# One remainder unit of 256 columns at the end, in place of two of 128, in a pooled attention with a multiplicative FFN

## The chip, the cores and the metric

The kernel runs on one core of a Trainium2 chip. The core has a matrix engine (TensorE, PE in the profile), a vector engine (VectorE, DVE), a scalar engine for activations (ScalarE, ACT), a general-purpose engine (GpSimd, POOL) and SyncE (SP), which here only issues transfers. Each runs its own instructions in order and waits for the others by semaphores. PE writes to PSUM, eight banks of 2 KB in each of 128 partitions; the other engines read the results from there.

The metric is the device time of one execution in microseconds, lower being better, as the median of several runs.

## The reference

Queries are averaged in neighbouring pairs, so that 1152 become 576. Attention follows, for 8 batches of 8 heads with 64 elements a head. Its output, 8 x 576 = 4608 tokens of 512 elements, goes through an FFN that multiplies two projections:

```
q_pool = q.reshape(B, H, S // 2, 2, D).mean(axis=3)
scores = matmul(q_pool, k.T) / sqrt(D)        # 576 x 1152 for each batch and head
attn   = softmax(scores)
x      = matmul(attn, v)                       # heads joined: (4608, 512)
a, b   = x @ w1, x @ w2                        # (4608, 1024)
out    = ((a * b) @ w3) @ w_out                # (4608, 512)
```

Inputs and output are float32; the kernel computes in float16 with float32 sums.

## The kernel before

**Attention.** Two heads of a batch form a pair P, 32 pairs in all, four to a batch. The scores of all pairs are one long sequence of columns, cut into 324 chunks of 512 columns. `scores(c)` (L294) computes a chunk on PE for both heads, one on each half of PE's rows, into a PSUM tile `psc`. `expo(c)` (L300) takes the exponential on ACT and writes it to the ring `er`. For a pair, `attend(P, u)` (L312) is called twice, once for each head, and multiplies the exponentials with the values. 576 is 4 x 128 + 64: the last 64 tokens of a batch, its remainder, are done for both heads in the call with u = 0 (L321). `normalize` divides and writes the tokens as `xn` (DVE), and SP's transposing DMAs bring them to `xT`, a batch's 512 main tokens. The remainders go through `rems` to `xR[:, head pair, batch // 2, head, 64]`, the even batches on partitions 0 to 63 and the odd ones on 64 to 127.

**FFN.** w3 and w_out are multiplied together once, early (T16, L477), so that the FFN is a gate and a row product. A `unit` is the FFN of a set of tokens. Its gates work on row tiles: h = 0 and h = 1 use the two 64-row halves of PE at once, each on other tokens. For each of 8 column tiles ft and each h, a gate is 16 matmuls of n columns (L514), 8 with w1 and 8 with w2, into one PSUM tile `pg`. Then one half is copied to `asb` (L497 on DVE, or L494 on ACT at the end) and DVE multiplies both into `gT[h]` (L506). The rows follow (L535): for each block of 128 tokens 16 matmuls of 512 columns, 8 on row tile 0 and then 8 on row tile 1, into `pp`, which is scaled into `osb` (L528, or L524 on ACT at the end) and stored by SP (L600). For a unit marked `final` the row blocks are kept back in the list `last` and run after everything else, with all 128 rows of PE at once; the very last block is cut into two halves (`last_rows`, L608).

**Units.** Every batch has a unit with n = 256, its main tokens. Remainders are grouped: with batch 3 comes a unit with n = 128 for the remainders of batches 0 to 3, and with batch 7 one for batches 4 to 7, which is `final`. `add_batch` puts the gates of the two units into one order, four of the main unit first and then mixed.

**Order of the work.** The program text is laid out by a planner in the kernel's own Python, with a model clock for each row tile, costs for each kind of instruction and due times. Chunks of scores come when their due time (the modelled end of the exponential two chunks ahead) is reached. Before that, `step(h)` fills the time with work of the queues `prep[h]` and `ffn[h]`. The FFN of a batch enters its queues once the attention of that batch has been issued, and its gates may start only when the model clock has passed `ready`, 6.5 us after the last u = 0 normalization (8.0 for the first two batches; L334). Row tile 0 may run ahead of row tile 1 by LEAD = 2.6 us of FFN work. The row products hand a PSUM tile from one row tile to the other through a tiny DVE copy (L434). After the last scores and attention blocks, `tail` is set: two more PSUM banks are used and ACT takes over copies. PE executes all of it in this fixed order.

The transfers are in three queues: loads of q, k, v and weights on POOL's, transposes and most stores on SP's, and two of the last stores on ACT's. Besides these, each engine's instructions are fetched by DMA (q8 and q14 in the profile).

Of the kernel before, what the change touches and what calls it, by code (L numbers as in the profile page):

```python
# [8 lines left out]
FP16 = mybir.dt.float16  # L9
# [14 lines left out]
def kernel(  # L24
# [17 lines left out]
    NF = dff // 128  # L42
# [9 lines left out]
    ffp = ctx.enter_context(tc.tile_pool(name="ffp", bufs=2))  # L52
# [4 lines left out]
    xR = const.tile([128, H // 2, 4, 2, 64], FP16)  # L57
# [26 lines left out]
    def vector(n, at):  # L84

        nonlocal vec
        vec = max(vec, at + T_SEM) + 0.16 + n / 960
        return vec
# [7 lines left out]
    def take():  # L96
        return spare.pop(0)[1]
# [311 lines left out]
    w3T = {}  # L409
# [31 lines left out]
    def add(queue, block, cost, ready, emit):  # L441


        for h in block.tiles:
            for n in range(block.n_products):
                queue[h].append((block, n, cost, ready(n) if callable(ready) else ready, emit))
# [34 lines left out]
    def unit(n, x, places, ready, final=False):  # L481

        gT = {}
        gdone = [[[1e9] for _ in range(NF)] for _ in range(2)]
        pairs = places[0][2][0][0] == places[0][2][1][0]

        def gate(ft, h):
            def mul(t, at):  # L490
                asb = ffp.tile([128, 256], FP32, tag="asb", bufs=3, name="asb")
                b, a = t[:, n:2 * n], asb[:, 0:n]
                if tail:
                    nc.scalar.copy(out=a, in_=t[:, 0:n])  # L494
                    at += 0.4
                else:
                    nc.vector.tensor_copy(out=a, in_=t[:, 0:n])  # L497
                    vector(n, at)
                if h not in gT:
                    gT[h] = ffp.tile([128, NF, n], FP16, tag="g" if n == 256 else "w3T",  # L500
                                     bufs=4, name="gT")
                g = gT[h][:, ft, 0:n]
                if pairs:
                    g = g.rearrange("f (i p c) -> f i c p", p=64, c=2)
                    b, a = (y.rearrange("f (i c p) -> f i c p", c=2, p=64) for y in (b, a))
                nc.vector.tensor_mul(out=g, in0=b, in1=a)  # L506
                done = vector(n, at)
                gdone[h][ft][0] = done + T_SEM
                return done
            fs = slice(ft * 128, ft * 128 + 128)  # L510

            def emit(t, s, i, start, stop):
                w, m = divmod(i, H)
                nc.tensor.matmul(t[:, n * w:n * w + n], (w1sb, w2sb)[w][s, (m + h) % 2, m // 2, fs],  # L514
                                 x(s, m),
                                 start=start, stop=stop, skip_group_check=True)
            add(ffn, Block("pg", 2 * H, (h,), mul), 0.0025 + n / 2400,
                [ready, copied[2 * ft // NF]], emit)

        def rows(h, o, places):  # L520
            def store(t, at):
                osb = ffp.tile([128, dm], FP32, tag="osb", bufs=3, name="osb")
                if tail:
                    nc.scalar.activation(out=osb, in_=t, func=AF.Copy, bias=0.0,  # L524
                                         scale=1.0 / (SCL * SCL))
                    done = at + T_SEM + 0.65
                else:
                    nc.vector.tensor_scalar_mul(out=osb, in0=t, scalar1=1.0 / (SCL * SCL))  # L528
                    done = vector(512, at)
                store_rows(osb, places)  # L530
                return done
            cs = slice(o, o + 128)

            def emit(t, s, i, start, stop):
                nc.tensor.matmul(t, gT[h][s, i, cs], T16[s, i, :], start=start, stop=stop,  # L535
                                 skip_group_check=True)
            if final:
                last.append((emit, store, places, lambda i: gT[h][:, i, cs]))
            else:
                add(ffn, Block("pp", NF, (0, 1), store), 0.216,  # L540
                    lambda i: [gdone[h][i]], emit)

        yield gate
        for h, o, to in places:
            rows(h, o, to)

    def add_batch(b, ready):

        k, o, end = (b // 2) % 2, 256 * (b % 2), b == B - 1
        units = [unit(256, lambda s, m: xT[s, m, k, o:o + 256],  # L550
                      [(h, 128 * i, [(b, 4 * i + 2 * h), (b, 4 * i + 2 * h + 1)])
                       for h in range(2) for i in range(2)], ready)]
        if b % 4 == 3:
            units.append(unit(
                128, lambda s, m: xR[s, m // 2, b // 2 - 1:b // 2 + 1, m % 2],
                [(h, 0, [(b - 3 + h, 8), (b - 1 + h, 8)]) for h in range(2)], ready, final=end))
        gates = [next(u) for u in units]
        for h in range(2):
            order = [(ft, gates[0]) for ft in range(NF)]
            for ft in range(NF if len(gates) > 1 else 0):  # L560
                order.insert(4 + 3 * ft // 2, (ft, gates[1]))
            for ft, gate in order:
                gate(ft, h)
        for u in units:
            next(u, None)
# [32 lines left out]
    def store_rows(osb, places):  # L598
        for r, rows in rows_out(places, slice(0, dm)):
            nc.sync.dma_start(out=rows, in_=osb[r])  # L600
# [76 lines left out]
    while c < NCHUNK or bursts or ffn[0] or ffn[1]:  # L677
        h = 0 if clock[0] <= clock[1] else 1
# [7 lines left out]
        if c >= NCHUNK or due(c) > clock[h]:  # L686
            fresh = False
            if c >= NCHUNK and not tail and not bursts:
                tail = True
                spare += [(max(clock), 4), (max(clock), 5)]  # L690
            keep = 1 if prep[0] or prep[1] or bursts and c > bursts[0][0] - 1 else 0
            if not step(h):
                if swap_due():
                    clock[:] = [max(clock) + 0.1] * 2
                    swap_halves()
                    clock[:] = [clock[0] + 0.1] * 2
                else:
                    clock[h] += 0.02
            while ended and not early and not prep[0] and not prep[1]:
                b, ready = ended.pop(0)  # L700
                add_batch(b, ready)
            continue
# [9 lines left out]
        if jobs:  # L712
            n, job = jobs.pop(0)
# [6 lines left out]
        while events and at >= events[0][0]:  # L720
            _, n, act = events.pop(0)
# [14 lines left out]
    for emit, store, _, _ in last[:-1]:  # L736
        n = take()
# [35 lines left out]
```

## Time and profile before

| | before |
|---|---|
| median of 3 runs | 421.24 us (420.91 to 422.11) |
| span of the profiled execution, first to last instruction | 423.3 us |
| PE busy with matmuls | 403.7 us, 7666 matmuls |
| ACT busy | 331.1 us, 308.8 of it with 324 exponentials |
| DVE busy | 218.9 us |
| narrow gates (xR, 128 columns) | 512 matmuls, first at 219.3, last at 406.9 us |
| last attention block on PE ends | 372.8 us |

The profile gives the profiled execution's own time only as its span; it is 2.1 us above the median of the runs, and none of those is named as the one that was profiled. A matmul's duration in the profile (216 ns with 128 columns, 269 with 256) includes its way through the array, and consecutive ones overlap; the pace is read from the starts. "Issue" ahead of an instruction means that the engine stood still though no semaphore that the profile shows was pending.

### The profile page before, as it was taken

The numbers are of one execution on the slowest core, as the hardware profiler recorded it, in microseconds if no ns is written. First come the engines' busy times: TensorE is split into PE (matmuls) and PEld (weight loads), VectorE is DVE, ScalarE is ACT, GpSimd is POOL, SyncE is SP. The second block draws the span as 40 slices with busy tenths as digits, with TensorE's granted clock in tenths as the row PEclk, the third lists the DMA queues.
The fourth block names the chain that finished last, engine by engine and source line by source line (L and its number), as shares of the span: only waits on it lengthen the run. The fifth ranks groups of instructions, "written<-read, shape, count | busy, mean of one in ns | idle before, by whom it ended". The sixth has DMA issues, their size and how long they took to land.

```text
span 423.3 us, 17431 instructions
## 1 busy us (share of the span) xinstructions
PE 403.7 (95%) x7666; PEld 318.0 (75%) x7666; DVE 218.9 (52%) x596; ACT 331.1 (78%) x382; POOL 191.2 (45%) x209
## 2 busy tenths in 40 slices
PE   3799999998999999999999899999999999999996
PEld 1366665777768887888788786788878887888993
DVE  2266656875435653565365663356446644542540
ACT  3968888887788888888888788889888888834432
POOL 8233345860566576555655556665569300000000
PEclk9999999999899999999999999999999999999999
DMA  8999999999699999999999999999996215102004
GB/s 120 206 207 202 186 205 204 189 161 121 110 154 206 152 141 153 196 144 121 192 170 132 139 134 132 190 185 150 137 170 141 42 35 133 43 19 101 4 11 141
DMA packets 94219, 59.02 MB, mean 139 GB/s; under 512 B 64832, under 2 KB 84544, under 8 KB 94144
## 3 DMA queue, kind: packets, MB, share of 16 engines
q0 software_dynamic: 26528, 33.56, 50.7%
q1 hardware_dynamic: 67456, 24.22, 35.1%
q8 instruction: 60, 0.98, 1.0%
q10 hardware_dynamic: 160, 0.13, 0.1%
q14 instruction: 15, 0.12, 0.1%
HBM read 67.11 MB, written 9.44 MB: 181 GB/s over the span
## 4 chain that ended last, share of the span: by engine, by line
PE 93%; ACT 3%; issue 2%; DMA 1%; DVE 0%; POOL 0%; DVEq 0%; ACTq 0%; POOLq 0%
PE pg L514 30%; PE psc L294 19%; PE po L312 18%; PE pp L535 15%; PE pT L477 4%; PE po L321 3%; ACT er L300 3%; PE t L262 1%; PE sw L391 1%; DMA kst<-in_k_dram 1%; PE w3t L465 0%; PE pp L608 0%; PE tb L195 0%; POOL qst L108 0%; ACT kc L207 0%
## 5 line engine op out<-in xcount | busy, mean ns | idle before, releaser
L300 ACT ACTIVATE er<-psc 128x1024 f16<-128x1024 f32 x324 | 308.8, 1030 | 52.0 <-PE psc L294 48.7
L294 PE MATMUL psc<-qT,kT 64*128 64x384 f16 (+7 forms) x1152 | 132.3, 291 | 4.6 <-ACT er L300 3.8
L514 PE MATMUL pg<-xT,w2sb 64*128 64x256 f16 x1024 | 131.3, 270 | 0.0
L514 PE MATMUL pg<-xT,w1sb 64*128 64x256 f16 x1024 | 130.7, 271 | 0.1
L514 PEld LDWEIGHTS <-w1sb 64*128 64x128 f16 x1280 | 97.9, 94 | 10.9 <-issue 2.7
L514 PEld LDWEIGHTS <-w2sb 64*128 64x128 f16 x1280 | 96.7, 94 | 6.2 <-issue 0.4
L535 PE MATMUL pp<-T,gT 64*128 64x512 f16 (+1 forms) x552 | 94.4, 376 | 0.0
L312 PEld LDWEIGHTS <-er 128*128 128x128 f16 x2304 | 74.5, 98 | 17.6 <-issue 15.0
L294 PEld LDWEIGHTS <-kT 64*128 64x128 f16 x1152 | 60.6, 95 | 32.5 <-issue 16.8
L312 PE MATMUL po<-vt,er 128*128 128x65 f16 x2304 | 82.4, 194 | 2.0 <-issue 1.8
L506 DVE TENSOR_TENSOR gT<-pg,asb 128x256 f16<-128x256 f32 (+1 forms) x160 | 66.3, 417 | 20.8 <-ACT asb L494 16.3
L497 DVE COPY asb<-pg 128x256 f32<-128x256 f32 (+1 forms) x119 | 48.0, 404 | 32.1 <-PE pg L514 30.5
L340 DVE RECIPROCAL rz<-po 128x4 f32<-128x4 f32 x64 | 12.1, 189 | 89.7 <-PE po L312 46.0
L143 POOL TENSOR_TENSOR qp<-qst 64x1152 f16<-64x1152 f16 x23 | 54.5, 2370 | 1.0
L535 PEld LDWEIGHTS <-gT 64*128 64x128 f16 (+1 forms) x552 | 41.3, 94 | 13.8 <-issue 0.4
L168 POOL COPY seen<-kT 1x1 f16<-1x1 f16 x19 | 3.4, 180 | 88.0 <-DMA kT<-kc 88.0
L152 POOL COPY vt<-vst 128x1152 f16<-128x1152 f16 x28 | 32.1, 1150 | 4.6 <-issue 3.9
L123 POOL DMA_DIRECT2D vst<-in_v_dram x32 | 23.3, 729 | 17.2 <-DMA kst<-in_k_dram 7.4
L116 POOL DMA_DIRECT2D kst<-in_k_dram x33 | 24.0, 729 | 11.7 <-issue 3.0
L343 DVE TENSOR_TENSOR xn<-po,rz 128x256 f16<-128x256 f32 x64 | 27.2, 424 | 2.2
L494 ACT COPY asb<-pg 128x256 f32<-128x256 f32 (+1 forms) x41 | 12.8, 332 | 19.4 <-PE pg L514 18.9
L161 POOL COPY kc<-kst 128x1152 f16<-128x1152 f16 x23 | 26.9, 1169 | 0.0
(62 smaller groups left out, 256.2 us busy)
## 6 DMA issues: line engine op xcount, KB each, us to landing
qst<-in_q_dram POOLq DMA_DIRECT2D x32, 288.0 KB, 6.0
vst<-in_v_dram POOLq DMA_DIRECT2D x32, 288.0 KB, 8.2
kst<-in_k_dram POOLq DMA_DIRECT2D x31, 288.0 KB, 5.4
out_dram<-osb SPq DMA_DIRECT2D x32, 256.0 KB, 3.2
w3h<-in_moe_w_dram POOLq DMA_DIRECT2D x4, 512.0 KB, 15.6
wosb<-in_moe_w_out_dram POOLq DMA_DIRECT2D x1, 1024.0 KB, 13.8
xT<-xn SPq DMA_TRANSPOSE x64, 5.8
w1sb<-in_moe_w_dram POOLq DMA_DIRECT2D x2, 512.0 KB, 15.9
```

The costliest lines, as they stand in the source:

```text
L116: nc.gpsimd.dma_start(out=kst[P][:, :, js[0]:js[1], :], in_=k[b, h0:h0 + 2].rearrange("u (p j) d -> p u j d", j=NJ)[:, :, js[0]:js[1], :])
L143: (eng or nc.vector).tensor_tensor(out=qps[pp][r].rearrange("p c u d -> p u c d"), in0=src[:, :, :, 0, :], in1=src[:, :, :, 1, :], op=ALU.add)
L152: (eng or nc.vector).tensor_copy(out=vts[P % 4][:, :, :, 0:D], in_=vst.pop(P))
L161: nc.gpsimd.tensor_copy(out=kc.rearrange("p j u d -> p u j d"), in_=kst.pop(P))
L294: nc.tensor.matmul(t[:, u, o:o + ln], kT[P][s, j, :], qv[s, f0:f0 + ln], start=True, stop=True)
L300: nc.scalar.activation(out=er[:, :, r:r + CH], in_=psc.pop(c), func=AF.Exp, bias=0.0, scale=SCALE)
L312: nc.tensor.matmul(po[:, VW * i:VW * i + D + 1], er[:, u, r:r + 128], vts[P % 4][:, u, j, 0:D + 1], start=(j == 0 and i == 0), stop=(j == ...
L343: nc.vector.tensor_tensor(out=xn, in0=acc[:, 0:4, 0:D], in1=rz[:, 0:4].to_broadcast([128, 4, D]), op=ALU.mult)
L497: nc.vector.tensor_copy(out=a, in_=t[:, 0:n])
L506: nc.vector.tensor_mul(out=g, in0=b, in1=a)
L514: nc.tensor.matmul(t[:, n * w:n * w + n], (w1sb, w2sb)[w][s, (m + h) % 2, m // 2, fs], x(s, m), start=start, stop=stop, skip_group_check=True)
L535: nc.tensor.matmul(t, gT[h][s, i, cs], T16[s, i, :], start=start, stop=stop, skip_group_check=True)
```

## The change

The unit of remainders that came with batch 3 is dropped. With batch 7 comes one unit for the remainders of all eight batches, with n = 256. On row tile h its columns are the remainders of batches h, 2 + h, 4 + h and 6 + h. It is marked `final`, so that all its four row blocks are in the list `last`, where there were two. The number of columns, multiplications and output rows is the same. Its `gT` takes buffers of the tag "g", where the narrow units took those of "w3T".

```diff
                 if h not in gT:
-                    gT[h] = ffp.tile([128, NF, n], FP16, tag="g" if n == 256 else "w3T",
-                                     bufs=4, name="gT")
+                    gT[h] = ffp.tile([128, NF, n], FP16, tag="g", bufs=4, name="gT")
...
-        if b % 4 == 3:
+        if end:
             units.append(unit(
-                128, lambda s, m: xR[s, m // 2, b // 2 - 1:b // 2 + 1, m % 2],
-                [(h, 0, [(b - 3 + h, 8), (b - 1 + h, 8)]) for h in range(2)], ready, final=end))
+                256, lambda s, m: xR[s, m // 2, :, m % 2],
+                [(h, 128 * i, [(4 * i + h, 8), (4 * i + 2 + h, 8)])
+                 for h in range(2) for i in range(2)], ready, final=True))
```

## The prediction

> **What bounds the kernel now.** I read the page first: its busy row and its slices say that TensorE (PE) has hardly an idle slice, while the exponentials on ScalarE (ACT) take 78%.
>
> ```profile
> span 423.3 us, 17431 instructions
> PE 403.7 (95%) x7666; PEld 318.0 (75%) x7666; DVE 218.9 (52%) x596; ACT 331.1 (78%) x382; POOL 191.2 (45%) x209
> PE   3799999998999999999999899999999999999996
> q8 instruction: 60, 0.98, 1.0%
> ...
> L514 PEld LDWEIGHTS <-w1sb 64*128 64x128 f16 x1280 | 97.9, 94 | 10.9 <-issue 2.7
> ```
>
> So the question is what PE does when. The chain in order of time shows the end. The last attention block ends at 372.8; all that follows is FFN back to back: the rest of batch 6, then the gates of batch 7 mixed with those of the second remainder unit (387.78 to 406.4 and a little beyond), then output rows.
>
> ```profile
> 371.00 1.39 PE po L312 x40
> 372.80 5.57 PE pg L514 x100
> 380.77 4.61 PE pp L535 x42
> 387.78 18.65 PE pg L514 x382
> 408.79 8.85 PE pp L535 x61
> 417.64 1.76 PE pp L608 x16
> ```
>
> Third, PE's timeline around the first remainder unit (batches 0 to 3, in the FFN of batch 3), with the first gate of batches 4, 6 and 7 on row tile 0.
>
> ```profile
> 226.43 0.22 PE L514 MATMUL pg<-xR,w2sb 64*128 64x128 f16 x1
> 226.44 0.22 PE L514 MATMUL pg<-xR,w1sb 64*128 64x128 f16 x1
> 226.49 0.22 PE L514 MATMUL pg<-xR,w2sb 64*128 64x128 f16 x1
> 226.50 0.22 PE L514 MATMUL pg<-xR,w1sb 64*128 64x128 f16 x1
> ...
> 230.27 0.23 PE L514 MATMUL pg<-xR,w1sb 64*128 64x128 f16 x1 [0.68 <-issue]
> ...
> 242.09 0.23 PE L514 MATMUL pg<-xR,w1sb 64*128 64x128 f16 x1 [1.45 <-issue]
> ...
> 271.16 0.27 PE L514 MATMUL pg<-xT,w1sb 64*128 64x256 f16 x1
> ...
> 352.56 0.27 PE L514 MATMUL pg<-xT,w1sb 64*128 64x256 f16 x1
> ...
> 385.11 0.38 PE L514 MATMUL pg<-xT,w1sb 64*128 64x256 f16 x2
> ```
>
> Two things are to be seen. A 128-column matmul follows the last one of its row tile after 0.055 us, half of the 0.109 us of a 256-column one (373.07, 373.18, 373.29 in the same view), so the narrow form wastes almost nothing. And inside the narrow stretch PE stops for "issue", with no semaphore pending: 0.84, 1.65 and 0.51 us beyond the usual step at 230.27, 242.09 and 252.84, together 3.0. From 110 to 218 and from 255 to 369, with 256-column gates alone, there is no such stop; before that there are two (0.29 at 88.96, 1.98 at 103.52).
>
> Last, windows from one batch's first gate on row tile 0 to the next one's (batches 3, 4, 5, and 6 up to the last scores), counting the gates alone:
>
> ```profile
> 206.90:271.00 64.10, 29.29 (x512) 22.25 (x64) 0.00 (x0) 1.00 1.04 150
> 271.00:313.20 42.20, 20.11 (x258) 13.38 (x32) 0.00 (x0) 1.00 1.09 163
> 313.20:352.50 39.30, 20.17 (x256) 13.97 (x32) 0.00 (x0) 1.00 0.49 87
> 352.50:369.30 16.80, 10.28 (x133) 5.73 (x14) 0.00 (x0) 1.00 0.26 83
> ```
>
> The FFN of a plain batch takes some 40.7 us between attention work. A batch's attention takes longer: the u=0 remainder matmuls of its last pair (L321) start at 198.27, 245.17, 289.24 and 333.66, 44.3 apart once the stops are taken out. So FFN work is not endless: only the first remainder unit makes the queue run late.
>
> **Gates.** Removed: 2 units x 2 row tiles x 8 column tiles x 16 matmuls of 128 columns (the 512 of the two xR groups); added: 256 of 256 columns. On a row tile one narrow unit costs 128 x 0.0555 = 7.1 us, two 14.2. The wide form on xR (four runs of 64 columns) is not in the trace: the xT gates' step gives 128 x 0.1095 = 14.0, twice the narrow step 14.2. I take 14.0, as the same shape. Merging alone is worth 0.2 us; moving is what counts. 7.1 us leave the middle, and the tail grows by 14.0 - 7.1 = 6.9.
>
> **Rows.** Two blocks of batches 0 to 3 leave the middle and join the last ones: 8 full-height matmuls of 512 columns at 0.2165 each, 1.73 a block, 3.46 in all. Their stores: ACT needs 0.60 a block (L524) and SP two issues of about 0.55 (L600) in 1.73 us, so they stay behind PE; without that cover they would cost at most 2 x 0.60. The last block, which alone sets the end, is built as before.
>
> **Covered.** In the middle DVE loses 16 copies and 16 products (286 and 290 ns) and two 691 ns evictions, SP four stores; PE did not wait for them (past the start its waits are for ACT, by the scores, and for issue). In the tail ACT's copy of 373 ns and DVE's product of 449 replace two of 267 and 290, each beside 0.875 us of PE for a gate. The g buffers that the wide unit takes are batch 6's, read out by then.
>
> **The middle.** Row tile 0 starts batch 3 at 206.9; its 61.1 us without stops hold 31.5 us of FFN work (20.9 of its own: 128 x 0.1095 + 32 x 0.2165; 10.6 moved), so without the unit it ends after 61.1 x 20.9/31.5 = 40.6, at 247.5. Batch 4 may start only at the planner's due time, 6.5 us after the normalization of its last u=0 block, which the code's costs end 1.07 after the matmuls: 7.6 in all. All later times have the stops before them taken out. Batch 4: 245.6 - 2.5 + 7.6 = 250.7; batch 5: 289.65 - 3.0 + 7.6 = 294.25; batch 6: 334.1 - 3.0 + 7.6 = 338.7. Each time row tile 0 is done 2 to 4 us earlier and stands dry. Hence batch 6 has 338.7 to 366.3 before the last scores, 27.6 x 0.51 (8.5 us of work in 16.8 above) = 14.1 of its 20.9, and 6.8 left at the attention's end, against 385.11 - 372.73 = 12.4 now. Batch 7's own due time comes 7.6 after that end: this is later, PE waits 0.8 for it, and it sets the start. Of the 10.36 (6.9 + 3.46) put on the tail, 12.4 - 7.6 = 4.8 is won back.
>
> **Stops.** Page row q8 has 60 packets for PE's 15332 instructions, 256 each; the packet records put one at 238.75 (2.07 us long), in the 242.09 stop. Narrow gates use up instructions twice as fast. Bounds: all 3.0 goes, or nothing. I take 2.6, nearest to the 256-column stretches: they had 2.3 us of stops in about 255 us from 75 on, 0.4 in the 40 us concerned.
>
> The section Instruction fetch mechanics of Runtime: NRT & Kernel Launch (the Trainium skill) has refills of 16 KiB, 256 instructions, "mostly hidden". The size agrees with the row; by the hiding the stops would have another cause and stay, and the sum would be 426.8.
>
> **Sum.** +10.4 - 4.8 - 2.6 = +3.0 us. Against the profiled span that is 426.3; that span lies 2.1 over the median of the runs (421.24), and carried over to the median it gives **424.2**.
>
> **Rivals.**
> - *The stops stay*, as fetches merely fall late elsewhere: 421.24 + 5.6 = 426.8. For it: the two stops before 104 without narrow gates. Against: none in 222 us later on.
> - *Within 0.3%.* Where both row tiles are dry, attention runs at ACT's pace. In ACT's timeline six exponentials take 5.75 us (0.958 a chunk) against 1.085 of PE work; with gaps I estimate 0.6 per 10.85 us. At most 10 us dry win 0.55; all stops gone wins 0.4; the wait for batch 7 covered, 0.8: 422.5. Against: tile 1 trails tile 0 by about 2.5 us of work, so both are rarely dry.
> - *Faster: the narrow stretch costs more than its stops show.* Late fetches may delay more than PE's gaps tell, scores and exponentials after them. The stretch (186 to 217 of 324 chunks) must then give back 6.9 us, not 2.6, to end at 419.9. Chunk starts there exceed the listed PE work by 3.5 us, which speaks against it.
> - *Faster: weight loads set the narrow pace.* With the 94 ns of the page's LDWEIGHTS row for each load, a narrow unit would take 128 x 0.094 = 12.0 us, the tail would grow by 14.0 - 12.0 = 2.0 instead of 6.9, and the time be 419.3. Against: the 0.055 us step, with a load to each matmul; loads overlap. TensorE: Matmul & The Clock Gate (the Trainium skill), section LDWEIGHTS, gives columns / 1.2 ns, 107 for these 128; by that figure a narrow unit would take 13.7 and the time be 417.6. The step contradicts that too.
> - *No gain in the middle*: later batches start no earlier, and batch 7 again 12.4 after the attention: 429.0. Against: the due times above.
> - *The clock drops in the new wait.* After the 1.81 us stop at 101.7 the granted clock was 0.50 from 105 to 108, which cost 1.6; after 1.45 at 242 it stayed at 1.00. With 0.8 us it should not: 425.8 if it does.
>
> **How the numbers follow.** The forecast holds 0.50 (423 to 425.5), the stops 0.17, within 0.3% 0.15, the late fetches 0.06, the weight loads 0.02, no gain 0.06, the clock 0.04. 0.3%, about what a measurement can tell, is 1.26 us: under 419.98 is faster (0.06 + 0.02 = 0.08), over 422.5 slower (0.50 + 0.17 + 0.06 + 0.04 = 0.77), 0.15 between. The range 421.0 to 427.2 takes in the near ones and the stops, leaving out faster, no gain and edges.
>
> **What would show it.** Steps hold if xR gates (256 of them, 64x256) run after the attention only, step 0.109; the attention's last block ends 2 to 3 us earlier with no "issue" stops from 219 to 253; batch 7's first gate comes 7 to 8 us after it; from there to PE's end is 44.7 us instead of 34.3. Wrong: stops at other places, batch 6 still at work 10 us after the attention, or an attention over 4 us shorter.

## The result, and the profile after

The changed kernel takes 427.24 us (median of 4 runs, 425.4 to 430.02) against 421.68 for the kernel before (420.91 to 424.84): 1.0139 times as long, with a 95% interval of 1.010 to 1.0178. Two later comparisons gave 1.0108 (1.0068 to 1.0149) and 1.0093 (1.0064 to 1.0122). It is slower, by about 1%. The forecast was 424.2, with a range up to 427.2; the first median lies just beyond its edge, the two later ones (425.45 and 425.58) within. One of the 68 runs of the kernel before (427.17 us, over 1.5% above the fastest of its set) counts as slow and is left out of the mean below.

The chain in order of time, end of the changed kernel (start us, us, what):

```profile
367.57 1.39 PE po L312 x40
369.37 7.32 PE pp L534 x56
378.22 26.38 PE pg L513 x482
406.12 13.43 PE pp L534 x81
419.56 1.76 PE pp L608 x16
```

The attention ends at 369.4, 3.4 us earlier than in the profile of before. Then come the rest of batch 6, gates up to 406 and the longer row part. From the attention's end to PE's end it is 51.9 us, where it was 46.6 (372.80 to 419.39). Of these 5.3 us more, the profiled spans show only 1.9 (425.2 against 423.3), because the attention of this execution ended earlier.

PE's timeline of the changed kernel: batch 3's first gate on row tile 0, then the stretch ahead of batch 4's, then the first gates of batches 5, 6 and 7.

```profile
203.88 0.27 PE L513 MATMUL pg<-xT,w1sb 64*128 64x256 f16 x1
...
243.95 0.38 PE L534 MATMUL pp<-T,gT 64*128 64x512 f16 x1
244.10 0.45 PE L294 MATMUL psc<-qT,kT 64*128 64x128 f16 x3
244.39 0.59 PE L534 MATMUL pp<-T,gT 64*128 64x512 f16 x2
244.74 0.35 PE L294 MATMUL psc<-qT,kT 64*128 64x448 f16 x1
244.82 0.38 PE L534 MATMUL pp<-T,gT 64*128 64x512 f16 x1
...
247.22 0.28 PE L513 MATMUL pg<-xT,w1sb 64*128 64x256 f16 x1
...
292.51 0.27 PE L513 MATMUL pg<-xT,w1sb 64*128 64x256 f16 x1
...
337.41 0.28 PE L513 MATMUL pg<-xT,w1sb 64*128 64x256 f16 x1
...
376.41 0.39 PE L513 MATMUL pg<-xT,w1sb 64*128 64x256 f16 x2
```

Between 244.4 and 247 the only FFN work is the row products of one row tile, one every 0.2 us or slower, where both tiles together had one every 0.108 (10 in 1.08 us from 241.03). That is a dry spell: row tile 0 has nothing until 247.22. Batch 7's first gate comes 7.0 us after the attention, where it was 12.3 (385.11 - 372.80).

Windows between these first gates, the gates alone (us, PE, DVE, ACT busy with counts, granted clock, DMA share, GB/s):

```profile
203.88:247.22 43.34, 19.93 (x257) 13.64 (x32) 0.00 (x0) 1.00 1.10 159
247.22:292.51 45.29, 18.09 (x257) 13.12 (x32) 0.00 (x0) 1.00 1.11 150
292.51:337.41 44.90, 18.05 (x256) 13.86 (x32) 0.00 (x0) 1.00 0.79 129
```

Without the narrow unit each batch's FFN takes as long as the attention of a batch (43 to 45 us, with 1.0 and 1.4 us of stops in the second and the third), not the 40.7 that it took while its queue never ran dry.

One more thing shows in the two profiles. Batch 3's first gate, up to which both programs are the same, is at 206.82 before and 203.88 after. PE's timeline of the kernel before, the long stop and that gate:

```profile
103.52 1.02 PE L312 MATMUL po<-vt,er 128*128 128x65 f16 x28 [1.81 <-issue]
...
206.82 0.27 PE L514 MATMUL pg<-xT,w1sb 64*128 64x256 f16 x1
```

So 2.9 of the 3.4 us by which the attention ends earlier were there before the change could act: that execution of the kernel before had the stop at 103.52, with a granted clock of 0.50 behind it.

### The profile page after: what moved, and what is told of

The parts are those of the page before. It is cut to its first block, busy times and chain, and to the rows that moved or that the text cites. A ratio compares the mean times of both kernels' runs of the same rounds, so it can differ in the third digit from the quotient of the medians.

```text
span 425.2 us, 16841 instructions
## 1 busy us (share of the span) xinstructions
PE 407.5 (96%) x7394; PEld 314.3 (74%) x7394; DVE 212.1 (50%) x568; ACT 330.0 (78%) x376; POOL 191.5 (45%) x209
## 4 chain that ended last, share of the span: by engine, by line
PE 92%; DMA 3%; ACT 2%; issue 1%; POOL 1%; DVE 1%; DVEq 0%; ACTq 0%; SPq 0%; POOLq 0%
PE pg L513 29%; PE psc L294 19%; PE po L312 18%; PE pp L534 16%; PE pT L477 4%; PE po L321 3%; DMA qst<-in_q_dram 2%; ACT er L300 2%; DMA qT<-qp 1%; PE t L262 1%; PE sw L391 1%; PE w3t L465 0%; PE pp L608 0%; POOL kst L116 0%; DVE qp L143 0%
## 5 line engine op out<-in xcount | busy, mean ns | idle before, releaser
L294 PE MATMUL psc<-qT,kT 64*128 64x384 f16 (+7 forms) x1152 | 134.3, 290 | 5.4 <-ACT er L300 3.8
L513 PE MATMUL pg<-xT,w2sb 64*128 64x256 f16 x1024 | 120.8, 269 | 0.0
L513 PE MATMUL pg<-xT,w1sb 64*128 64x256 f16 x1024 | 119.8, 269 | 0.1
L513 PEld LDWEIGHTS <-w1sb 64*128 64x128 f16 x1152 | 85.5, 94 | 7.3 <-issue 0.4
L513 PEld LDWEIGHTS <-w2sb 64*128 64x128 f16 x1152 | 85.8, 94 | 5.3
L505 DVE TENSOR_TENSOR gT<-pg,asb 128x256 f16<-128x256 f32 x144 | 62.6, 444 | 22.2 <-ACT asb L494 18.4
L497 DVE COPY asb<-pg 128x256 f32<-128x256 f32 x111 | 46.7, 421 | 28.6 <-PE pg L513 27.6
L340 DVE RECIPROCAL rz<-po 128x4 f32<-128x4 f32 x64 | 12.1, 189 | 92.8 <-PE po L312 48.4
L534 PEld LDWEIGHTS <-gT 64*128 64x128 f16 (+1 forms) x536 | 38.6, 94 | 21.6 <-issue 0.8
L494 ACT COPY asb<-pg 128x256 f32<-128x256 f32 x33 | 10.8, 374 | 19.6 <-PE pg L513 18.5
```

Source lines behind the costliest of these rows:

```text
L294: nc.tensor.matmul(t[:, u, o:o + ln], kT[P][s, j, :], qv[s, f0:f0 + ln], start=True, stop=True)
```

## The experiments

The tail, from the end of the last attention block to PE's end, is the same to 0.01 us in the three profiles of the kernel before and in the three of the changed kernel, so it is the measure wherever the question is the order of the work. Theory A in the expectations is that the tail is the whole effect and the stops are accidental; theory B that narrow gates bring the stops.

**The kernel before, unchanged.**

> The kernel before, unchanged, with a second profile. Theory A (the stops of PE in the first profile were an accident of that execution, which was slower than the median): ratio to before 1.00, and the stretch of the narrow gates of batch 3 (some 219 to 253 us) shows less than 1 us of 'issue' stops; the stop near 103 us is gone or elsewhere. Theory B (narrow gates use up instructions faster than they are fetched): again about 3 us of stops in that stretch. Both: 46.6 us from the end of the last attention block on PE to PE's end.

> The kernel before, a third profile. Theory A (each execution is the program's time without stops, with PE's last attention block ending at 366.2 us and PE's end 46.6 later, plus the stops that the execution happens to have): the attention ends at 366.2 plus the stops that the trace lists, within 0.4. Theory B (the narrow gates of batch 3 always cost 3 us): again 3 us of 'issue' stops between 215 and 253 us, as in the two profiles so far, whatever the execution's time.

Measured: 421.25 us (ratio 1.000, 0.9972 to 1.0028) and a single 420.10. PE's timeline of the first of the two:

```profile
227.26 0.23 PE L514 MATMUL pg<-xR,w1sb 64*128 64x128 f16 x1 [0.75 <-issue]
239.35 0.23 PE L514 MATMUL pg<-xR,w1sb 64*128 64x128 f16 x1 [1.72 <-issue]
```

and of the second:

```profile
236.90 0.23 PE L514 MATMUL pg<-xR,w1sb 64*128 64x128 f16 x1 [0.47 <-issue]
```

Theory A missed the first: beyond PE's usual step these stops are 0.91 and 1.92, with one of 0.23 some ten us later 3.1 in all, in the same places as in the first profile. Only the stop near 103 us is gone, as it had expected. Theory B missed the second: 0.68 in all. The places are fixed and the size is not. The attention ends at 370.6 and 367.6; with the listed stops (4.1 and 1.1) taken out that is 366.5 both times. The tail is 46.6 in each.

**The changed kernel, unchanged.**

> The changed kernel, unchanged, timed with more rounds. Theory A: what is deterministic is the tail, 51.9 us from the last attention block to PE's end against 46.6, and the middle gives nothing back: +5.3, ratio 1.012 to 1.014, 426.5 to 427.5. Theory B: stops saved in the middle are real, ratio about 1.006, 424.

> The changed kernel once more, for a narrower interval and a third profile. If the whole effect is the tail (51.93 against 46.59) and the stops come to about the same in both kernels: 5.3 us, ratio 1.0125. If taking the narrow gates out of the middle saves stops of 2.6 us on the average, as the prediction had it: 2.7 us, ratio 1.0065. The attention's last block ends at 366.2 to 366.5 us plus the stops that the trace lists.

Measured: 425.45 us (1.0108) and 425.58 (1.0093), between the two expectations; the intervals are too wide for either comparison to decide alone. The tail is 51.93 in both, as in the first profile. Stops are there too, in other places. PE's timeline of the second, and then of the changed kernel's first profile:

```profile
264.13 0.19 PE L321 MATMUL po<-vt,er 128*64 128x65 f16 x1 [1.08 <-issue]
```

```profile
262.81 0.19 PE L321 MATMUL po<-vt,er 128*64 128x65 f16 x1 [0.53 <-issue]
...
311.73 0.31 PE L294 MATMUL psc<-qT,kT 64*128 64x320 f16 x2 [1.10 <-DMA qT<-qp]
```

So without narrow gates PE stops in an attention block (0.7 to 1.2 us beyond the usual step in the three profiles), and in the first one also for a transposed qT that landed late. With the listed stops taken out, the attention ends at about 367, where 366.2 to 366.5 was expected: the count of listed stops leaves up to 1 us unexplained.

**The move without the merge**: both remainder units keep 128 columns, and both come with batch 7.

```diff
-        if b % 4 == 3:
+        for q in (0, 2) if end else ():
             units.append(unit(
-                128, lambda s, m: xR[s, m // 2, b // 2 - 1:b // 2 + 1, m % 2],
-                [(h, 0, [(b - 3 + h, 8), (b - 1 + h, 8)]) for h in range(2)], ready, final=end))
+                128, lambda s, m, q=q: xR[s, m // 2, q:q + 2, m % 2],
+                [(h, 0, [(2 * q + h, 8), (2 * q + 2 + h, 8)]) for h in range(2)], ready,
+                final=True))
...
+            if len(gates) > 2:
+                order = [e for x in order for e in (
+                    (x, (x[0], gates[2])) if x[1] is gates[1] else (x,))]
```

> The move without the merge: both remainder units have 128 columns and both come with batch 7, four row blocks at the end. Theory A (the move costs all, the merge is worth 2 x 7.1 - 14.0 = 0.2): as the changed kernel or 0.2 over it, tail 51.9 to 52.3. Rival (the wide form is what costs or saves, by weight loads or by its reads of xR): over 1 us from the changed kernel either way; by weight loads of 94 ns it would be slower than the changed kernel by 2 x 12.0 - 14.0 = 10 us.

Measured: 427.09 us (1.0137, 1.0097 to 1.0178), tail 52.25, so 0.3 us over the changed kernel's tail. The merge is worth that little, and the move is the whole loss. Had weight loads set the narrow pace, it would be some 10 us slower than the changed kernel, as the expectation says. In this program 128-column gates fill the tail, where the DMA engines are nearly idle (share 0.02 from 380 to 402), and no "issue" stop occurs among them.

**The narrow unit of batches 0 to 3 with a later batch**, 4, 5 or 6 in place of 3 (the diff is for 5):

```diff
-        if b % 4 == 3:
+        if b in (5, B - 1):
+            q = 2 if end else 0
             units.append(unit(
-                128, lambda s, m: xR[s, m // 2, b // 2 - 1:b // 2 + 1, m % 2],
-                [(h, 0, [(b - 3 + h, 8), (b - 1 + h, 8)]) for h in range(2)], ready, final=end))
+                128, lambda s, m: xR[s, m // 2, q:q + 2, m % 2],
+                [(h, 0, [(2 * q + h, 8), (2 * q + 2 + h, 8)]) for h in range(2)], ready, final=end))
```

> The unit of batches 0 to 3, narrow as before, comes with batch 5 in place of batch 3. Theory A (work removed from the middle lets row tile 0 stand dry ahead of a batch's due time): dry ahead of batch 4 (3.2 us, 1.6 us of work) and batch 5 (about 3 us, 1.5 of work), none later; the tail grows by 3.1 to 49.7, ratio 1.007, 424.6. Rival (the middle has no slack, order is free): ratio 1.00, tail 46.6. Theory B: the narrow stretch, now some 300 to 345 us, has 3 us of 'issue' stops.

> The unit of batches 0 to 3, narrow, comes with batch 4. Row tile 0 is dry ahead of batch 4 alone. From narrow_b5 (tail 50.2, two dry spells, 3.6 us) each spell costs 1.8 us: tail 48.4 us. Rival (order is free): 46.6. If the stops come with narrow gates under a loaded DMA: 'issue' stops of about 3 us between 260 and 300 us; if they are accidental: any amount.

> The unit of batches 0 to 3, narrow, comes with batch 6. Three dry spells of row tile 0, 1.8 us each: tail 46.6 + 5.4 = 52.0 us, as much as in the changed kernel though 10.4 us of the work stand ahead of batch 7. Rival (what costs in the changed kernel is the work behind batch 7's gates): tail 46.6 to 50.2.

| narrow unit of batches 0 to 3 comes with | 3 (before) | 4 | 5 | 6 | 7 (two narrow) | 7 (one wide) |
|---|---|---|---|---|---|---|
| tail, us | 46.6 | 48.6 | 50.2 | 52.1 | 52.3 | 51.9 |

The variant with batch 5 was timed in several runs: 423.2 us, 1.0062 (1.0031 to 1.0093); those with 4 and 6 only once each (424.28 and 424.31). Tails of 48.4, 49.7 and 52.0 were expected. Up to batch 6, each batch that passes without the extra work costs 1.6 to 2.0 us, as the dry spells say, and the order is not free; the last step, from 6 to 7, adds only 0.2. With batch 6 the tail is as long as the changed kernel's though the unit's gates stand ahead of batch 7: what was lost in the middle does not depend on where the work goes later. On the stops: with batch 5 the narrow gates, from 303.6 us on, bring none; with batch 4 the trace lists 0.27, 0.18 and 1.36 between 263 and 286, all in attention blocks, and 0.68 at 217 in wide gates. The 1.36 falls among the narrow gates of that stretch, so this run decides nothing; the one with batch 5 shows that narrow gates do not bring stops as a rule.

**The due time**, in the changed kernel and, as a control, in the kernel before:

```diff
-            ended.append((b, [vec + (8.0 if b < 2 else 6.5)]))
+            ended.append((b, [vec + (8.0 if b < 2 else 4.5)]))
```

> The changed kernel with the planner's due time of a batch's FFN 4.5 us after the last normalization in place of 6.5. Theory A (row tile 0 waits for due times, in the middle and ahead of batch 7): batch 6 ends 1.0 us of work earlier, batch 7's first gate comes 5.5 us after the attention in place of 7.0: tail 50.4, time 1.5 us below the changed kernel's, ratio to before 1.008. Rival (the transposed tokens land too late, or the wait does not bind): PE stands still for the landing, tail 51.9, ratio 1.011.

> The kernel before with the due time 4.5 in place of 6.5 us, as a control. Theory A: there the due times of batches 4 to 7 do not bind, as row tile 0 always has work: tail 46.6 as before. Rival (an earlier due time helps whatever the backlog): tail about 45 us.

The changed kernel with the earlier due time: 423.2 us (1.0049, 1.0021 to 1.0076, where 1.008 was expected) and a tail of 50.0, 1.9 less; batch 7's first gate comes 5.8 us after the attention. The control's tail is 46.6, unchanged (its single time, 425.28, has 6.7 us of stops and waits in it, 2.0 of them for w1sb at 81; two stops in its narrow stretch come to 2.8). So the due time binds only where the queue is dry. It can be moved too far, though, as PE's timeline of the changed kernel with 4.5 shows:

```profile
247.43 0.27 PE L513 MATMUL pg<-xT,w1sb 64*128 64x256 f16 x1 [1.12 <-DMA xT<-xn]
```

Batch 4's gates started at 245.07 and PE then stood for tokens that had not landed, which holds up attention as well.

No variant comes below the kernel before. The tails fit the middle: there row tile 0 always has work, and what the variants change is how much of it they lose.

## Why the prediction was wrong, by its steps

- **Gates and rows: right.** From batch 7's first gate to PE's end 44.7 us were expected; it is 44.9 (376.41 to 421.3). The merge was put at 0.2 us; the tails say 0.3. The wide xR gates have the mean of 269 ns of the xT gates.
- **The middle: right.** Batch 4's first gate was expected at 250.7; it comes at 247.22, and 2.9 us must be added as this execution was that much ahead when batch 3 began: 250.1. The first gates of batches 4 to 7 follow the last attention block of their own batch by 6.8 to 7.6 us (7.6 expected). Of 10.4 us moved, 4.8 was to be won back; the tail grew by 5.3, so 5.0 was.
- **The stops: wrong.** This is the step that failed: "I take 2.6, nearest to the 256-column stretches". It counted stops of one execution in one stretch as the price of the narrow gates, and took other stretches of the same execution as the measure of a kernel without them. The narrow stretch does hold stops in all four profiles of that order of work (3.0, 3.1, 0.7 and, in the control, 2.8), so they are not nothing. But when it went, other places stopped, which the prediction itself had named as a sign of being wrong.

How much was really saved can be told from the times. Without stops the attention would end at about 366.2 (so it did in narrow_b5, which had none after 53 us; in two_narrow_end, whose work up to there is the changed kernel's, it was 366.4). With the tail, 3.9 us from PE's end to the last instruction and 1.8 between span and time (424.25 against 422.5 in two_narrow_end), an execution without stops would take 366.2 + 46.6 + 3.9 + 1.8 = 418.5 before and 366.2 + 51.9 + 3.9 + 1.8 = 423.8 after. The fastest runs seen are 418.87 and 423.68. The mean of 67 runs of the kernel before is 421.6, so they lose 3.1 us to stops, to transfers that land late and to starts that differ; all 16 of the changed kernel have 426.1, so 2.3. What is given back is 0.8 us, not 2.6; with standard errors of the two means of 0.2 and 0.4, nothing at all is not excluded. With it the change comes to 5.3 - 0.8 = 4.5 us; the three comparisons of medians show 3.9 to 5.6. The six profiles of the two unchanged programs say the same of the middle alone: from the first attention call of batch 4 to the last of batch 7 they take 166.4, 167.3 and 164.5 us before, 165.9, 164.5 and 165.1 after, 0.9 less on the average.

What the stops are can be read from the traces, too. Take PE's matmuls and weight loads in the order of their starts and count them in blocks of 256, for each of which queue q8 brings one packet of 16,384 bytes (60 packets in the kernel before, 58 in the changed one). All 32 "issue" stops of more than 0.06 us in the twelve profiles, narrow gates or not, fall on the same place of a block to within one instruction (taken here for its border), and PE goes on 1.3 to 1.8 us after a packet of q8 has landed (2.9 in one case, the stop at 103.52). So these stops are waits for PE's next instructions. One at some 53 us is in eleven of the twelve profiles, in both kernels alike. In the kernel before the long ones among the narrow gates are at the borders of blocks 31 and 33; the changed kernel passes these two without a stop, and stops at 262 to 264 at the border of block 36, in an attention block, which the kernel before passes. So the prediction had the right kind of cause; what it missed is that the new order of the work has a late border of its own.

- **Carrying over to the median: a weak point of the same kind.** The profiled execution of before ended 2.1 us over the median even as a span, and had 6.6 us of stops and their consequences (372.8 - 366.2). A saving that is read off such an execution cannot be taken in full from a median one.
- **The rivals.** "The stops stay", as fetches fall late elsewhere (426.8, given 0.17), is the one that came out, nearly: 0.8 of its 2.6 us went. The half clock did not come: in the changed kernel's first profile PE goes from batch 6's last products to batch 7 with the clock at 1.00, and there was no wait in which both row tiles stood still. "Weight loads" fell with the 0.3 us of the merge. That the DMA's load decides on a stop fits, but was not tested by itself: the narrow gates without stops had less of it (a share of 0.02 in two_narrow_end's tail, 0.45 and 0.18 from 310 to 330 us in narrow_b5, 1.04 in the stretch of before), and there each packet had landed 2.8 us or more before its block was needed. But narrow_b5 also passed one border among narrow gates, at 308 us, without a stop under a share of 1.18. Why a packet is sometimes late, and by how much, stays open.

## What to carry to other kernels

Where a planner fills the gaps of one stage with the work of another, the amount of work still waiting is itself a resource: taking a piece out of the middle is free only as long as the next piece may already start, so compare each batch's end with the next one's due time before moving anything to the tail. Read small stalls off several executions, and take the shortest run as the program and the rest as its stalls; then a term like "these stops go away" can be sized by an average instead of by the one execution that was profiled. Merging two narrow matmul streams gains only what their starts show, here 0.3 us out of 14.

## What was not expected

A program's stops keep their places from one execution to the next, borders of its instruction blocks, while their sizes change (0.7 to 3.1 us in one stretch); a program that differs only in the order of its work has other work at these borders and stops elsewhere, in attention blocks at 262 to 264 us. PE's work is so full that each stop moves the end by nearly its own length: taking the stops out leaves an attention that ends at 366 to 367.5 us in every program with the due time of 6.5 us.
